# A two-level Strassen-Winograd channel MLP: the transposes of its input move from TensorE to VectorE

## The chip, the cores and the metric

The kernel runs on one core of one Trainium2 chip. A core has TensorE (PE: matmuls, and weight loads shown as PEld), VectorE (DVE), ScalarE (ACT), GpSimd (POOL), SyncE (SP, which only issues transfers here) and 16 DMA engines. The metric is the device time of one execution in microseconds (us), the median of several runs.

## The reference, cut to what matters

All data are fp32. Attention without softmax over 8 batches, 8 heads, 576 tokens and 64 columns a head gives x; then a token-mixing MLP and a channel MLP follow:

```
kv  = einsum('bhsd,bhse->bhde', k, v)
o   = einsum('bhsd,bhde->bhse', q, kv)
x   = o / sqrt(mean(o*o) + 1e-6) * g_norm           # heads side by side: (8, 576, 512)
u   = x + (relu(x.T @ w_tok1) @ w_tok2).T            # w_tok1 (576, 256), w_tok2 (256, 576)
out = u + relu(u @ w_ch1) @ w_ch2                    # w_ch1 (512, 1536), w_ch2 (1536, 512)
```

The change is in the last line, the channel MLP, which fills most of the time.

## The kernel before, in words

**First pass.** Attention and token mixing run over pairs of batches. VectorE meanwhile decodes the weights (rounds of small integer and float steps). The result u goes to DRAM in nine groups of 512 tokens by 512 columns (`u_dram[0..8]`): the first 512 tokens of each batch, and a ninth group of the 64 left over of all eight.

**Second pass.** For each group, `channel1` forms v = relu(u @ w_ch1) and `channel2` adds v @ w_ch2 to u. Both products use the Strassen-Winograd scheme: 7 block products in place of 8, with sums of blocks before and after. For group 0 one level is used (`channel1_once`, `channel2_once`), and at the same time VectorE makes the sums of weight blocks that the later groups need, and they are stored in DRAM. For groups 1 to 8 two levels are used: 7 outer products, each of 7 inner ones. An inner product is three matmuls of 128x128x128.

**Places.** The order of groups 1 to 8 is written by hand. An inner product has a place, a whole number: outer product number n starts at place 7n, and its inner products 1, 2, 6, 5, 7, 4, 3 stand at 7n + 0, 1, 3, 4, 6, 9, 12 (`PLACE`), so that consecutive outer products interlock and each place has one inner product. A group takes 14 outer products, so 98 places: a cycle. Everything else is put beside a place with `put`: the loop at the end of the kernel emits the product of a place and then what stands beside it, and each engine keeps this program order. `channel2` of a group begins 49 places after its `channel1`; in the text, places count from the start of `channel1`'s cycle, and `b` in the code is the first place of the half concerned.

**Banks of an outer product** (`outer`). Inner products 1, 6, 7 and 4 add up in PSUM bank "a". Between them the bank is read: t1 after 1, u2 after 6, u3 after 7, the result (1,0) after 4. Such a read is a copy by ACT, or, where a block of another outer product is to be added (`base`), an add by VectorE. Product 2 has bank "c", 5 and 3 share bank "b"; VectorE adds t1, u2, u3 to them (`write`).

**Sums.** `inner(o)` makes the sums of v's blocks that outer product o of `channel2` needs (tiles sv, sv3; VectorE). S1 to S4 and A21 (`sum1` to `sum4`, `make_a21`) are the outer sums of v, each in two halves of 768 elements. `radd` and `xadd` gather the result tiles r into xg, which holds u and becomes the output. POOL makes two of v's outer sums. `fetch_sums` loads the weight sums of outer product n + 3 after product n (three buffers).

**Transposes.** The channel product needs u with columns on partitions. `fetch_t` loads 128 tokens of a group, `turn_u` transposes them by four TensorE transposes into PSUM (`ps_ut`, line 515) and ACT copies them into uT. For group g + 1 that happens within `channel2` of g, at its places 11, 15, 19 and 23. `outer_u` and `inner_u` then form the sums of uT's blocks (VectorE).

**Queues.** In the second pass all transfers are issued by SyncE, in program order.

Of the kernel before, what the change touches and what calls it, by code (L numbers as in the profile page):

```python
# [19 lines left out]
def kernel(  # L20
# [481 lines left out]
    def fetch_t(g, i):  # L502

        if g < NG:
            xt[g, i] = late["xt"].tile([P, DM], F32, name="xt")
            dma(xt[g, i], u_dram[g][ts(i, P)])

    def turn_u(g, i, psum):
        if g >= NG:
            return  # L510
        if i == 0:
            uT[g] = late["u"].tile([P, 7, 7, P], F32, name="uT")
        pt = psum()
        for c in range(NC):
            keep(nc.tensor.transpose(pt[:, c], xt[g, i][:, ts(c, P)], ident))  # L515
        o, n = 2 * (i // 2), 2 * (i % 2)
        copy(uT[g][:, o:o + 2, n:n + 2], pt.rearrange("p (o n) t -> p o n t", o=2))

    def outer_u(g):

        return t_sums(lambda n: uT[g][:, SB[n], :4]) if g < NG else []

    def inner_u(g, lo, hi):

        return t_sums(lambda n: uT[g][:, lo:hi, SB[n]]) if g < NG else []
# [5 lines left out]

    def t_psum():
        return late["t"].tile([P, NC, P], F32, name="ps_ut")
# [20 lines left out]
    def channel1_once(g):  # L554
# [4 lines left out]
        def pair(d):  # L559
            a11, a12, a22, s1, s2, s3, s4 = (t[:, 2 * d:2 * d + 2] for t in blocks)  # L560
            shape = [P, 2, 2, P]

            def product(n, ps, start, stop):
                for w in range(2):
                    i, f = divmod(2 * d + w, W)
                    for c in range(2):
                        wt = w_ch1[:, SA[n]] if SA[n] < 4 else late["w2"][:, SA[n] - 4]
                        matmul(ps[:, w], lhsT=wt[:, 2 * i + c, ts(f, P)],
                               rhs=uT[g][:, SB[n], c:4:2],
                               start=(start and w == 0 and c == 0), stop=stop,  # L570
                               skip_group_check=True)

            at = {}

            def first():
                for n in ("t1", "u2", "u3"):
                    at[n] = r_tile().rearrange("p i (j t) -> p i j t", j=2)
                for n in (1, 6, 7, 5):
                    at[f"p{n}"] = m_psum(shape, f"ps_v{n}")
                product(1, at["p1"], True, False)  # L580
                copy(at["t1"], at["p1"])

            def sixth():
                product(6, at["p6"], True, True)
                tensor_add(at["u2"], at["p6"], at["t1"])

            def seventh():
                product(7, at["p7"], True, False)
                tensor_add(at["u3"], at["p7"], at["u2"])

            def fifth():
                product(5, at["p5"], True, False)
                tensor_add(a22, at["p5"], at["u3"])
                relu(a22, a22)

            def second():
                product(2, at["p1"], False, True)
                relu(a11, at["p1"])

            def fourth():  # L600
                product(4, at["p7"], False, True)
                tensor_add(a12, at["p7"], at["u2"])
                relu(a12, a12)

            def third():
                product(3, at["p5"], False, True)
                tensor_add(s3, at["p5"], at["u2"])
                v_sums(s1, s2, s3, a11, a22)
                v_sum3(s3, a11)
                tensor_add(s4, a12, s2, ALU.subtract)  # L610

            return [first, sixth, seventh, fifth, second, fourth, third]
# [63 lines left out]
    def outer(place, size, mul, to, base=None):  # L676
# [11 lines left out]
        def temp(n, bufs):  # L688
            t[n] = late["tmp"].tile([P, FQ], F32, name=n, tag=n, bufs=bufs)[:, :size]
            return t[n]  # L690

        def fit(flat, like):
            return flat if len(like.shape) == 2 else flat.rearrange("p (w t) -> p w t", w=W)

        def read(o, i, j):

            a = fit(banks["a"], to(i, j))
            o = fit(o, to(i, j)) if len(o.shape) == 2 else o
            if base:
                tensor_add(o, a, base(i, j))  # L700
            else:
                copy(o, a)

        def write(i, j, name, n):
            o = to(i, j)
            tensor_add(o, fit(banks[name], o), fit(t[n], o))
# [30 lines left out]
    ORDER1, ORDER2 = (1, 6, 2, 7, 5, 3, 4), (1, 4, 6, 5, 7, 2, 3)  # L737
# [3 lines left out]
    def fetch_sums(n):  # L741
        if n < len(order):
            w, _, o = order[n]
            sums[n] = sums_tile()
            dma(sums[n], sums_dram[w, o])
# [6 lines left out]
    def channel1(g, n0):  # L752
# [4 lines left out]
        def first(i, o):  # L757
            n = n0 + i

            def mul(p, ps, start, stop):  # L760
                for w in range(W):
                    matmul(ps[:, ts(w, P)], lhsT=part(1, o, p, sums[n])[:, ts(w, P)],
                           rhs=uT[g][:, SB[o], SB[p]], start=(start and w == 0), stop=stop,
# [18 lines left out]
        put(b + 24, *add(3, 3, 1))  # L782
        put(b + 36, *add(1, 4, 3, nc.gpsimd))
        put(b + 43, *add(7, 5, 4, nc.gpsimd))
        for t, *places in ((2, 25, 29, 28, 25), (7, 47, 47, 48, 48), (1, 53, 57, 53, 54)):
            for place, (i, j) in zip(places, ((0, 0), (0, 1), (1, 0), (1, 1))):
                rectify(place, t, i, j)
        if g > 1:
# [4 lines left out]
    def channel2(g, n0):  # L793
# [3 lines left out]
        def second(i, o):  # L797
# [15 lines left out]
            outer(7 * n, P, mul, to)  # L813
# [3 lines left out]
        rs = {o: second(i, o) for i, o in enumerate(ORDER2)}  # L817

        def inner(o):
# [24 lines left out]
            return begin, steps[1], own if o == 1 else steps[2], steps[3]  # L844
# [5 lines left out]
        def sum1(i):  # L850
            keep(nc.vector.scalar_tensor_tensor(out=half(n5(), i), in0=half(a21(), i), scalar=0.0,
                                                in1=half(n4(), i), op0=ALU.max, op1=ALU.add))

        def sum2(i):
            tensor_add(half(n6(), i), half(n5(), i), half(n1(), i), ALU.subtract)

        def sum3(i):

            keep(nc.vector.scalar_tensor_tensor(out=half(n7(), i), in0=half(a21(), i), scalar=0.0,
                                                in1=half(n1(), i), op0=ALU.max, op1=ALU.subtract))  # L860

# [12 lines left out]
        for place, steps in (  # L874
                (-17, [ins[1][0], ins[1][2]]), (-16, [ins[1][1]]), (-14, [ins[1][3]]),
                (1, [A[0], ins[4][0]]), (2, [A[1]]), (4, [ins[4][1], S1[0]]), (6, [ins[4][3], S1[1]]),
                (7, [ins[4][2]]), (8, [S2[0]]), (9, [S2[1]]), (11, [ins[6][0]]), (12, [S4[0]]),
                (13, [ins[6][1], S4[1]]), (15, [ins[6][3], ins[6][2]]), (17, [ins[5][0], S3[0]]),
                (19, [ins[5][1], S3[1]]), (20, [xadd(0, 0, 1)]), (21, [ins[5][3], ins[5][2]]),
                (23, [ins[7][0], xadd(1, 0, 4)]), (25, [ins[7][1]]), (26, [ins[7][2], ins[7][3]]),  # L880
                (28, [ins[2][0]]), (29, [radd(6, 1)]), (30, [ins[2][1], xadd(0, 1, 6)]),
                (32, [ins[2][3], ins[2][2]]), (34, [ins[3][0]]), (36, [xadd(0, 1, 5), ins[3][1]]),
                (37, [xadd(1, 1, 5)]), (38, [ins[3][3], ins[3][2]]), (43, [radd(7, 6)]),
                (44, [xadd(1, 0, 7)]), (45, [xadd(1, 1, 7)])):
            put(b + place, *steps)

        if g < NG - 1:
            for place, steps in ((57, [do(store, g, xg, 1)]), (59, [xadd(0, 0, 2)]), (63, [xadd(0, 1, 3)]),
                                 (71, [do(store, g, xg, 0)]), (78, [do(fetch_x, g + 1, 0)]),
                                 (85, [do(fetch_x, g + 1, 1)])):  # L890
                put(b + place, *steps)
        else:
# [5 lines left out]
            put(b + 49, xadd(0, 0, 2), do(store, g, xg, 1))  # L898
# [5 lines left out]
        for i in range(J):  # L904
            place = b + 12 + 4 * i
            put(place - 12, do(fetch_t, g + 1, i)) if i < 2 else None
            put(place - 1, do(turn_u, g + 1, i, t_psum))
            put(place, do(fetch_t, g + 1, i + 2)) if i < 2 else None

        if g + 1 < NG:  # L910
            first, second, _, fourth = inner_u(g + 1, 0, 2)
            put(b + 40, first)
            put(b + 41, second)
            put(b + 42, fourth)
# [129 lines left out]
    late["xt"] = pool("xt", 2)  # L1044
    late["u"] = pool("u", 1)
    fetch_t(0, 0)
# [4 lines left out]
    def turn(g, i, psum):  # L1051
        turn_u(g, i, psum)
        if i + 2 < J:
            fetch_t(g, i + 2)

    u_psum = lambda: ps["o"].tile([P, NC, P], F32, name="ps_ut", tag="o")
    last = [
        "h00 2 -s40 2", "h01 2", "h10 2", "h11 2", "hr 1", "c0 u0 1", "c1 u1 1", "c2 u2", "c3 u3 1", "u4",
        "c4 u5 1", "u6 1", "u7", "u8"]
    more = {f"c{i}": do(turn, 0, i, u_psum) for i in range(J)}  # L1060
# [5 lines left out]
    right.close()  # L1066
    late["v"] = pool("v", 1, "right")
    late["r"] = pool("r", 4, "right")
# [5 lines left out]
    late["m"] = pool("m", 6, space=bass.MemoryType.PSUM)  # L1074
    late["t"] = pool("t", 2, space=bass.MemoryType.PSUM)
# [4 lines left out]
    fetch_t(1, 0)  # L1080
    fetch_t(1, 1)
# [3 lines left out]
    weave(channel1_once(0), firsts + [f for fs, _ in inner1 for f in fs])  # L1085
    for n in range(3):
        fetch_sums(n)
    extra = [do(turn, 1, i, t_psum) for i in range(J)]
    extra += [lambda: [f() for f in outer_u(1)], lambda: [f() for f in inner_u(1, 0, 7)], lambda: None]
    body = [step for pair in zip(channel2_once(0), extra) for step in pair]  # L1090
# [50 lines left out]
```

## Time and profile before

| | |
|---|---|
| time, median of 3 runs | 831.82 us (831.56 to 831.87) |
| profiled span | 830.2 us |
| second pass, from its first two-level product | 281 us to the end |
| one cycle (groups 1 to 7) | 67.8 us |
| VectorE busy in a cycle | 58.44 us |
| DMA share in a cycle | 0.52 |

Each line of the page's list of groups gives source line, engine, operation, output and inputs, shape and count, then busy us, mean ns of one, and idle time of the engine before them. As most operations are recorded by a few helpers, many groups share a line (127 matmul, 118 tensor_add, 124 copy); tile names tell them apart. An fp32 matmul shows as two records, a transpose as one. "Busy" counts overlapping instructions once, and a mean duration includes the latency that the next instruction overlaps; the price of an instruction in a full queue is the distance between starts.

### The profile page before, as it was taken

The numbers are of one execution on the slowest core, as the hardware profiler recorded it, in microseconds if no ns is written. First come the engines' busy times: TensorE is split into PE (matmuls) and PEld (weight loads), VectorE is DVE, ScalarE is ACT, GpSimd is POOL, SyncE is SP. The second block draws the span as 40 slices with busy tenths as digits, with TensorE's granted clock in tenths as the row PEclk, the third lists the DMA queues.
The fourth block names the chain that finished last, engine by engine and source line by source line (L and its number), as shares of the span: only waits on it lengthen the run. The fifth ranks groups of instructions, "written<-read, shape, count | busy, mean of one in ns | idle before, by whom it ended". The sixth has DMA issues, their size and how long they took to land.

```text
span 830.2 us, 16562 instructions
## 1 busy us (share of the span) xinstructions
PE 812.6 (98%) x6528; PEld 719.9 (87%) x6528; DVE 701.8 (85%) x1334; ACT 289.1 (35%) x777; POOL 76.9 (9%) x59
## 2 busy tenths in 40 slices
PE   6999999999999999999999999999999999999997
PEld 6655555644888899999999999999999999999997
DVE  4688989999785979978977987997897897798696
ACT  1346665562210124234234323322423322333321
POOL 1200101010000020003003003001100300300300
PEclk9999999999999999999999999999999999999999
DMA  9999996422436445365356446546536545644642
GB/s 296 325 341 319 337 364 244 153 89 102 174 127 220 175 169 170 118 194 200 128 165 216 144 141 204 181 140 193 192 115 191 185 149 145 216 164 141 190 144 80
DMA packets 67966, 156.57 MB, mean 189 GB/s; under 512 B 5296, under 2 KB 24752, under 8 KB 67888
## 3 DMA queue, kind: packets, MB, share of 16 engines
q1 hardware_dynamic: 66208, 153.77, 56.6%
q10 hardware_dynamic: 1680, 1.74, 0.7%
q8 instruction: 52, 0.85, 0.4%
q14 instruction: 26, 0.21, 0.1%
HBM read 128.35 MB, written 27.13 MB: 187 GB/s over the span
## 4 chain that ended last, share of the span: by engine, by line
PE 88%; DVE 9%; issue 1%; DMA 1%; ACT 1%; SPq 0%; ACTq 0%; DVEq 0%
PE ps_a L127 35%; PE ps_b L127 18%; PE ps_c L127 9%; PE ps_h L127 6%; PE ps_u L127 6%; PE ps_v L127 4%; PE ps_w L127 3%; PE ps_o L127 3%; PE ps_ut L515 2%; PE ps_kv L127 2%; DVE sv L118 1%; DMA raw<-in_moe_w_tok_dram 1%; DVE v L118 1%; DVE x L379 1%; DVE ms L399 1%
## 5 line engine op out<-in xcount | busy, mean ns | idle before, releaser
L124 ACT COPY u<-ps_a 128x128 f32<-128x128 f32 (+1 forms) x176 | 60.5, 344 | 176.5 <-PE ps_a L127 164.6
L118 POOL TENSOR_TENSOR v<-v,v 128x768 f32<-128x768 f32 x32 | 58.4, 1856 | 553.0 <-ACT t L124 553.0
L127 PE MATMUL ps_b<-uT,sums 128*128 128x128 f32 x672 | 85.5, 275 | 0.0
L127 PEld LDWEIGHTS ps_b<-uT,sums 128*128 128x128 f32 x672 | 80.2, 192 | 0.0
L127 PE MATMUL ps_a<-uT,w_ch 128*128 128x128 f32 x576 | 78.8, 275 | 0.0
L127 PEld LDWEIGHTS ps_a<-uT,w_ch 128*128 128x128 f32 x576 | 71.5, 192 | 0.1
L118 DVE TENSOR_TENSOR v<-ps_b,u 128x384 f32<-128x384 f32 x112 | 60.2, 550 | 12.9 <-PE ps_b L127 12.9
L127 PE MATMUL ps_u<-h,w_tok 128*128 128x512 f32 (+1 forms) x160 | 67.0, 601 | 0.0
L127 PE MATMUL ps_h<-x,w_tok 128*128 128x512 f32 (+1 forms) x160 | 65.8, 603 | 0.8 <-ACT x L424 0.8
L118 DVE TENSOR_TENSOR v<-v,v 128x768 f32<-128x768 f32 (+1 forms) x70 | 64.1, 926 | 0.3
L118 DVE TENSOR_TENSOR uT<-uT 128x512 f32<-128x512 f32 (+4 forms) x103 | 63.1, 628 | 1.1
L124 ACT COPY t<-ps_a 128x128 f32<-128x128 f32 (+1 forms) x88 | 30.3, 344 | 92.7 <-PE ps_a L127 85.3
L121 ACT ACTIVATE v<-v 128x384 f32<-128x384 f32 (+1 forms) x102 | 49.3, 526 | 30.7 <-DVE v L118 26.6
L127 PE MATMUL ps_a<-uT,w 128*128 128x128 f32 x432 | 58.7, 275 | 0.0
L118 DVE TENSOR_TENSOR u<-ps_a,v 128x384 f32<-128x384 f32 x48 | 26.8, 558 | 32.1 <-PE ps_a L127 31.6
L127 PEld LDWEIGHTS ps_h<-x,w_tok 128*128 128x128 f32 (+1 forms) x160 | 25.9, 189 | 31.9 <-issue 28.1
L127 PEld LDWEIGHTS ps_a<-uT,w 128*128 128x128 f32 x432 | 53.4, 192 | 0.0
L118 DVE TENSOR_TENSOR xg<-xg,r 128x512 f32<-128x512 f32 (+1 forms) x78 | 50.7, 661 | 0.8 <-ACT r L124 0.6
L424 ACT ACTIVATE x<-x,inv 128x64 f32<-128x64 f32 x184 | 46.0, 335 | 9.5 <-DVE inv L419 8.1
L127 PE MATMUL ps_a<-uT,sums 128*128 128x128 f32 x336 | 46.9, 276 | 1.3 <-ACT t L124 1.3
L127 PE MATMUL ps_a<-sums,sv 128*128 128x128 f32 x336 | 47.3, 277 | 0.9 <-ACT r L124 0.5
L127 PEld LDWEIGHTS ps_u<-h,w_tok 128*128 128x128 f32 (+1 forms) x160 | 24.5, 179 | 27.1 <-issue 22.4
(123 smaller groups left out, 1650.1 us busy)
## 6 DMA issues: line engine op xcount, KB each, us to landing
sums<-sums SPq DMA_DIRECT2D x112, 576.0 KB, 3.8
qT<-in_q_dram SPq DMA_DIRECT2D x8, 1152.0 KB, 9.5
xt<-u_dram SPq DMA_DIRECT2D x36, 256.0 KB, 3.5
xg<-u_dram SPq DMA_DIRECT2D x18, 512.0 KB, 4.9
k_in<-in_k_dram SPq DMA_DIRECT2D x16, 512.0 KB, 9.2
u_dram<-x SPq DMA_DIRECT2D x16, 512.0 KB, 3.6
out_dram<-xg SPq DMA_DIRECT2D x16, 512.0 KB, 5.4
sums<-sv SPq DMA_DIRECT2D x14, 576.0 KB, 2.8
```

The lines of the kernel that those rows point to most:

```text
L118: keep(engine.tensor_tensor(out=o, in0=a, in1=b, op=op))
L121: keep(nc.scalar.activation(o, a, AF.Relu))
L124: keep(nc.scalar.copy(o, a))
L127: keep(nc.tensor.matmul(*a, **kw))
L379: keep(nc.vector.tensor_mul(heads(X[pair, c][:, t]), heads(bank[c, t]), g_sb.to_broadcast([P, H, D])))
L399: keep(nc.vector.tensor_reduce(stats_of(c)[0][:, ts(t, H)], sq[c, t], axis=AX.X, op=ALU.add))
L424: keep(nc.scalar.activation(x[:, i], x[:, i], AF.Copy, scale=inv[:, i]))
L515: keep(nc.tensor.transpose(pt[:, c], xt[g, i][:, ts(c, P)], ident))
```

## The change

It takes the 36 x 4 transposes from TensorE. VectorE transposes blocks of 32x32 instead (two instructions for each of four quarters of a group), four transfers a quarter put these blocks into DRAM, and eight transfers a group bring them back so that the blocks stand as a whole transpose in uT. Rows of uT are thus split in four pieces of 32 tokens, and matmuls and sums read them so. The loads for it run far ahead: quarters are turned during `channel1` of the group before.

To make room on VectorE, the outer products of `channel2` come in the order 1, 2, 4, 7, 6, 5, 3 (before: 1, 4, 6, 5, 7, 2, 3), and those of `channel1` have 4 before 3. S3 is made first, S2 from S3, S1 from S2. Product 6 adds product 1's result as it reads its bank, which saves one `radd`. There are five result tiles in place of four; seven of the result additions, and the stores, move to the beginning of the next cycle. POOL makes one of its sums in quarters. The two PSUM banks of the transposes go to the products (8 in place of 6). The loads of weight sums are issued by ACT.

```diff
-            xt[g, i] = late["xt"].tile([P, DM], F32, name="xt")
-            dma(xt[g, i], u_dram[g][ts(i, P)])
+            xt[g, i] = late["xt" if g else "xt0"].tile([P, 2, DH], F32, name="xt")
+            dma(xt[g, i], u_dram[g].rearrange("(t p) e -> p t e", p=P)[:, ts(i // 2, 2), ts(i % 2, DH)])
-        for c in range(NC):
-            keep(nc.tensor.transpose(pt[:, c], xt[g, i][:, ts(c, P)], ident))
-        copy(uT[g][:, o:o + 2, n:n + 2], pt.rearrange("p (o n) t -> p o n t", o=2))
+        for t in range(2):
+            keep(nc.vector.transpose(
+                y[:, :, 2 * t:2 * t + 2].rearrange("p b n t -> p n b t"),
+                xt[g, i][:, t].rearrange("p (n b t) -> p n b t", n=2, b=NC)))
+        for a in range(NC):
+            dma(blocks_dram[g, half][:, :, o, a], y[ds(a * Q, Q)].rearrange("p b n t -> p b (n t)"))
+    def fetch_u(g, half):
+            uT[g] = late["u"].tile([P, 7, NC, 7, Q], F32, name="uT")
+        for b in range(NC):
+            dma(uT[g][ds(b * Q, Q), 2 * half:2 * half + 2, :, :4].rearrange("p o a n t -> p o a (n t)"),
+                blocks_dram[g, half][:, b])
...
-    ORDER1, ORDER2 = (1, 6, 2, 7, 5, 3, 4), (1, 4, 6, 5, 7, 2, 3)
+    ORDER1, ORDER2 = (1, 6, 2, 7, 5, 4, 3), (1, 2, 4, 7, 6, 5, 3)
-            dma(sums[n], sums_dram[w, o])
+            dma(sums[n], sums_dram[w, o], nc.scalar)
+        for place, f, i in ((18, turn_blocks, 0), (19, fetch_t, 1), (29, turn_blocks, 1), (30, fetch_t, 2),
+                            (40, turn_blocks, 2), (41, fetch_t, 3), (49, turn_blocks, 3), (70, fetch_t, 4)):
+            put(b + place, do(f, g + 1 + i // J, i % J))
+            outer(7 * n, P, mul, to, o == 6 and (lambda i, j: rs[1][0][:, i, ts(j, P)]))
...
+                (8, [A[0]]), (9, [A[1]]), (10, [ins[2][3]]), (11, [S3[0]]), (12, [S3[1]]),
+                (14, [ins[4][2]]), (15, [S2[0]]), (16, [ins[4][3]]), (17, [ins[7][0]]), (18, [xadd(0, 0, 1)]),
+                (19, [ins[7][1]]), (21, [S2[1], ins[7][2]]), (23, [ins[7][3]]), (24, [S1[0]]),
+            for place, steps in ((45, [xadd(0, 1, 6)]), (48, [radd(7, 6)]), (57, [xadd(1, 1, 5)]),
+                                 (59, [xadd(1, 0, 4)]), (60, [xadd(1, 0, 7)]), (61, [xadd(1, 1, 7)]),
+                                 (61, [do(store, g, xg, 1)]), (63, [xadd(0, 1, 5)]), (64, [xadd(0, 1, 3)]),
+                                 (66, [do(store, g, xg, 0)]), (74, [do(fetch_x, g + 1, 0)]),
...
+        put(b + 8, do(fetch_u, g + 1, 0))
+        put(b + 12, do(fetch_u, g + 1, 1))
-    late["r"] = pool("r", 4, "right")
+    late["r"] = pool("r", 5, "right")
-    late["m"] = pool("m", 6, space=bass.MemoryType.PSUM)
-    late["t"] = pool("t", 2, space=bass.MemoryType.PSUM)
+    late["y"] = pool("y", 1, "right")
+    late["m"] = pool("m", 8, space=bass.MemoryType.PSUM)
```

## The prediction

> **What bounds the kernel now.** I read the page's busy table and slices first, then the chain that ended last, then PE's timeline by stage, then VectorE's load by stage, then the transfers.
>
> ```profile
> PE 812.6 (98%) x6528; PEld 719.9 (87%) x6528; DVE 701.8 (85%) x1334; ACT 289.1 (35%) x777; POOL 76.9 (9%) x59
> ...
> PE 88%; DVE 9%; issue 1%; DMA 1%; ACT 1%; SPq 0%; ACTq 0%; DVEq 0%
> ```
>
> ```profile
> L515 PE MATMUL ps_ut<-ident,xt 128*128 128x128 f32 x144 | 21.7, 273 | 0.0
> ```
>
> ```profile
> 248.05 0.44 PE ps_ut L515 x4
> ```
>
> TensorE never rests and is 88% of the chain, so its instruction count sets the time. The second fence is the group of the 144 transposes (busy us, mean ns, idle before); the third is one entry of the chain in order of time (start, us): four transposes hold TensorE for 0.44 us. Their mean of 273 ns is a pipelined latency, not a price.
>
> The second pass repeats in cycles, one for each of groups 1 to 8. TensorE's timeline, around the transposes of one cycle:
>
> ```profile
> 457.05 0.83 PE L127 MATMUL ps_b<-sums,sv 128*128 128x128 f32 x6
> 457.72 0.60 PE L515 MATMUL ps_ut<-ident,xt 128*128 128x128 f32 x4
> 458.16 0.93 PE L127 MATMUL ps_b<-w_ch,sv 128*128 128x128 f32 x6
> 458.92 1.50 PE L127 MATMUL ps_a<-d,v 128*128 128x128 f32 x12
> ...
> 461.37 0.83 PE L127 MATMUL ps_a<-sums,v 128*128 128x128 f32 x6
> 462.25 0.91 PE L127 MATMUL ps_a<-sums,sv 128*128 128x128 f32 x6
> ```
>
> Columns: start, us, engine, line, operation, count, idle before and who ended it. A product of the inner scheme (a "place": three fp32 matmuls, six records) starts every 0.67 us. A cycle is 98 places x 0.67 = 65.68, plus 16 transposes at 4 x 0.435 = 1.74, plus starts that come late: 462.25 is 0.88 after 461.37 (0.21 lost), and the gaps after 458.16 and 462.25 are 0.76 and 0.75 (0.09, 0.08 lost). Sum 67.80, the period seen.
>
> The second engine is VectorE (DVE), by stretches of one such cycle:
>
> ```profile
> 387.00:407.40 20.40, 20.35 (x182) 20.11 (x181) 20.36 (x42) 6.89 (x21) 0.00 (x0) 1.00 0.49 161
> 353.40:387.00 33.60, 33.60 (x303) 33.60 (x302) 25.35 (x49) 12.18 (x28) 7.29 (x4) 1.00 0.61 198
> ```
>
> Columns: stretch, length, then busy us of PE, weight loads, DVE, ACT, POOL, clock, DMA share, GB/s. DVE is full (20.36 of 20.40) in the first part of the second product and has 8 us free in the first product. What that fullness costs is seen in the last cycle, which has no transposes in it:
>
> ```profile
> 797.11 0.94 PE L127 MATMUL ps_b<-w_ch,sv 128*128 128x128 f32 x6 [0.27 <-DVE r L118]
> ...
> 801.22 0.91 PE L127 MATMUL ps_a<-sums,sv 128*128 128x128 f32 x6 [0.49 <-ACT r L124]
> ```
>
> TensorE loses 0.43, 0.66 and 0.63 us there (starts against the 0.67 step), with 0.09 after each: 2.0 us. So taking the transposes out and nothing else would give back in stalls what it saves: 1.74 + 0.38 a cycle against 2.0. The reordering is the part that decides.
>
> **What the Trainium skill says.** "Perfetto Trace Analysis", Identifying the Most-Contended Engine, says that matmul busy overstates how full TensorE is and weight-load busy is better: here 98% and 87%, and the unbroken 0.67 us step agrees that nothing is left but to issue fewer instructions. "VectorE: DVE Perf Modes", The three transpose paths, says that VectorE transposes blocks of 32x32 only; hence the detour of the blocks through DRAM, which no trace here shows yet. "DMA: Bandwidth & Descriptors", Issuing engines are not separate DMA queues, says that loads issued by ACT share the engines with SyncE's and only save issue time; not shown before, since the second pass issues all on SyncE.
>
> **The change, part by part.**
>
> *Transposes and their copies leave TensorE and ACT.* 36 x 0.44 = 15.8 us on the path. With them goes the wait of 0.38 a cycle, in the seven cycles that have it: 2.7 us. 36 ACT copies (587 ns) go too; ACT is 35% busy, worth nothing by itself.
>
> *VectorE's load.* DVE prices from starts that follow each other:
>
> ```profile
> 796.30 0.55 DVE L118 TENSOR_TENSOR v<-v 128x384 f32<-128x384 f32 x1
> 796.77 0.28 DVE L118 TENSOR_TENSOR r<-ps_b,u 128x128 f32<-128x128 f32 x1
> 796.97 0.95 DVE L118 TENSOR_TENSOR v<-v,v 128x768 f32<-128x768 f32 x1
> 797.84 0.28 DVE L118 TENSOR_TENSOR r<-ps_c,t 128x128 f32<-128x128 f32 x1
> ```
>
> 384 elements occupy 0.47, 128 0.20, 768 0.87: 1.04 ns an element and 68 ns. A block transpose (8 a cycle, 256 elements of a partition each) is not in the trace. "Vector Engine (DVE) Microarchitecture Reference", 3.8 The reshape front-end, gives one element per cycle per lane: 0.34 us by the same line, my value. Upper bound 0.60, if four-byte data took two passes. A cycle gains 8 x 0.34, four adds of 128 in place of ACT copies in product 6 (0.80), and loses one add of 512 (0.60): 56.6 to 59.4 of 65.7 us.
>
> I laid each DVE instruction at the place where the code puts it and summed by stretch. Places 49 to 76 (second product, first part): before 20.8 us for 18.8 of matmuls and 1.7 of transposes; after 17.7 for 18.8. Seven result additions leave for places 8 to 15 of the next cycle, and S3, S2, S1 are spread over places 60 to 77. Places 7 to 27: before 10.5, after 13.6 of 14.1. So the stretch that starved TensorE is relieved, and the free one nearly filled. The last cycle's 2.0 us should go.
>
> *Where DVE now can hold TensorE.* Products 2, 5, 4 (and now 6) are read out of bank "a" by DVE, and the same bank is wanted three places later: 1.34 us, less the read's 0.56 and some 0.1 of hand-over, leaves 0.69 us of lateness. Following DVE's queue from place to place with these prices, the latest such reads are u2 at places 17 and 38, 0.6 us late: just inside. At 0.60 a transpose, place 38 is 1.05 late: 0.36 a cycle. I charge 0.15 x 8 = 1.2 us.
>
> *New waits.* DVE's transpose waits for its load (3.5 us median) and for the 4 stores of the one before, since there is one buffer of each; behind it in DVE's queue stand the writes and reads that TensorE's banks wait for. Transposes are 9 to 11 places (6 to 7.4 us) apart; 1.7 us of stores' issue and the load fit with 0.6 to 1 us over. The last one, at place 49, may be 0.7 late, where the reads that follow are ACT's. The eight loads of uT may start at place 57 at the earliest and are first needed at place 91: some 20 us, against 4 + 4 transfers of 3 to 5 us that overlap. ACT now issues the 14 loads of sums, each after the copy of u3; behind it stands the next copy of "a", 2 us later, and an issue is 0.32 us on SyncE. The sums (3.8 us to landing) have 11 places, 7.4 us, less that copy.
>
> *First pass and entry.* Eight transposes for group 0 (2.7 us) fall where DVE is 90% busy; sums of uT move behind u7. 0.5 us charged. The gap at the entry to the steady part:
>
> ```profile
> 285.74 0.83 PE L127 MATMUL ps_a<-uT,w_ch 128*128 128x128 f32 x6
> 287.86 0.94 PE L127 MATMUL ps_a<-uT,sums 128*128 128x128 f32 x6 [1.29 <-ACT t L124]
> ```
>
> is 1.45 us, and 0.1 after it: DVE's backlog of uT sums. They now come one product (5.6 us) earlier, into idle time of DVE. I count 1.0 us of it as gained.
>
> Five result tiles and eight PSUM banks let results live across the cycle; ordering 3 and 4 swapped costs nothing as long as POOL's four quarter sums (about 0.95 us each, half of 1856 ns) end before product 4 reads them, 1.3 us earlier by the same count. S1 and S2 from S3 are as many instructions of the same price.
>
> Sum: 15.8 + 2.7 + 2.0 + 1.0 - 1.2 - 0.5 = 19.8 us; 831.8 - 19.8 = 812.0.
>
> **Rivals.**
> *VectorE takes over.* For: 59.4 of 65.7 us, and 0.09 us in hand at place 17. Against: lateness stays under 0.69 up to a transpose of about 0.4. At 0.60, 0.36 x 8 = 2.9 us more: 815; at 1.0 (64.8 of 65.7) reads are 2.7 late, 2 us a cycle: 828.
> *The detour and the queues.* u goes out and in again, 2 MB a cycle in pieces of 512 bytes, DMA share 0.52 before. ACT's loads reuse semaphores of SyncE's transfers, and an ACT held there delays copies. If half of the gain of a cycle is lost so, 1.2 x 8: 822.
> *Slower.* If the sums land 1 us late for four products a cycle, 4 x 8 = 32: 844. If matmuls that read uT in pieces of 32 columns ran 10% longer (half of all, 32.8 us a cycle), 3.3 x 8 = 26: 838. Against both: 3.8 us against about 7, and pieces of 128 with gaps (ps_v, 380 ns for 256 columns) show no cost now.
>
> **How the numbers follow.** Forecast (809 to 815.5) 0.64; VectorE 0.17; queues 0.10; slower 0.07; below the 809.7 that is left if nothing is charged and all of the entry's gap goes (831.8 - 15.8 - 2.7 - 2.0 - 1.6), 0.02. The range runs from 808.5 to 822, taking in most of the first two rivals. Faster 0.91 and same 0.02, since a bad case of the queues can eat the whole gain; slower 0.07.
>
> **What would show it.** Right: period 65.7 to 66.0 us, no ps_ut, transposes near 0.34 from start to start, no PE wait for DVE at places 49 to 76. Wrong: a PE wait repeated each cycle on DVE u2 (places 17, 38), on DMA sums, or a step over 0.67 us for products on uT.

## The result and the profile after

The changed kernel takes 842.4 us (median of four runs, 838.2 to 844.7) against 831.7 before: 1.0123 times as long, 95% interval 1.0082 to 1.0163. The prediction was 812.0, faster. The profiled run took 838.2. The page of the changed kernel, busy table, then the chain that ended last, by engine and by line:

```profile
PE 807.2 (97%) x6384; PEld 707.4 (85%) x6384; DVE 730.0 (87%) x1430; ACT 255.1 (31%) x709; POOL 78.9 (9%) x75
...
PE 52%; DVE 28%; DMA 11%; issue 4%; SPq 4%; ACT 0%; ACTq 0%; DVEq 0%
PE ps_a L127 20%; PE ps_b L127 9%; DMA xt<-u_dram 6%; DVE uT L118 6%; PE ps_c L127 5%; PE ps_h L127 5%; DVE xg L118 4%; DVE v L118 4%; SPq L115 4%; PE ps_u L127 4%; DVE sv L118 3%; PE ps_w L127 2%; PE ps_o L127 2%; DVE r L118 2%; DMA v_in<-in_v_dram 2%
```

The 144 matmul records of the transposes are gone, and TensorE is still "97% busy". But its share of the chain fell from 88% to 52%: 28% of it is now VectorE's, and 11% that of transfers, first among them the load of xt, which was on no path before. The waits of VectorE (total us, times, longest) name it, and the group of the new transposes (busy, mean ns, idle before) shows how much:

```profile
DVE y L520 <- DMA xt<-u_dram: 25.3, 16, 4.0
```

```profile
L520 DVE STREAM_TRANSPOSE y<-xt 128x256 f32<-128x256 f32 x72 | 27.6, 421 | 28.5 <-DMA xt<-u_dram 25.3
```

They stand still as long (28.5 us) as they work.

Where the time went, from TensorE's starts (each start against the one before, less the 111.7 ns of an unhindered matmul record; that step is the same before and after, also for products on uT):

| part of the span | before | after | difference |
|---|---|---|---|
| 144 transposes, 109 ns each | 15.7 | 0 | -15.7 |
| TensorE's late starts from the first product of ps_a on | 7.2 | 22.4 | +15.2 |
| length of the ps_v part (first products of group 0) | 36.4 | 40.6 | +4.3 |
| last start of TensorE to the end | 4.9 | 6.9 | +2.0 |
| sum | | | +5.8 |

The span grew from 830.2 to 836.1 us, 5.9. The other three runs of the changed kernel, 3.9 to 6.5 us longer, were not profiled; their granted TensorE clock was 0.996, 0.996 and 0.993, against 0.999 in this one, which would be 5 of the 6.5 us in the longest (an estimate from these figures: 0.006 of 838 us).

In the repeated part the gaps sit at fixed products. They are counted here by TensorE's products from the start of a cycle; the places in the code and in the prediction are two higher, so product 18 is the code's place 20. In us a cycle: 0.71 at products 17 and 18 (in all cycles but the first), 1.0 at 36 to 39, 0.24 at 50. Irregular ones come at 32, 42, 52 and 71 (5.7 us in all). One cycle (start, us, operation, count, idle before and its cause; count the start against 0.67 us a product):

```profile
498.62 0.83 PE L127 MATMUL ps_b<-uT,sums 128*128 128x128 f32 x6
499.64 0.94 PE L127 MATMUL ps_b<-uT,sums 128*128 128x128 f32 x6 [0.19 <-DVE v L118]
500.57 1.60 PE L127 MATMUL ps_a<-uT,w_ch 128*128 128x128 f32 x12
```

```profile
513.00 0.94 PE L127 MATMUL ps_a<-uT,sums 128*128 128x128 f32 x6
513.78 1.66 PE L127 MATMUL ps_b<-uT,sums 128*128 128x128 f32 x12
515.89 0.94 PE L127 MATMUL ps_a<-uT,w_ch 128*128 128x128 f32 x6 [0.46 <-DVE u L118]
```

From 498.62 to 499.64 are 1.02 us for one product; from 513.78 to 515.89 are 2.11 for two. The cause named at these products is VectorE, never a transfer. VectorE's timeline of the second stretch:

```profile
508.48 0.77 DVE L520 STREAM_TRANSPOSE y<-xt 128x256 f32<-128x256 f32 x2 [0.55 <-DMA xt<-u_dram]
...
512.40 0.55 DVE L118 TENSOR_TENSOR t<-ps_a,v 128x384 f32<-128x384 f32 x1
512.87 1.11 DVE L118 TENSOR_TENSOR sv<-v,sv 128x384 f32<-128x384 f32 x1
...
515.29 0.54 DVE L118 TENSOR_TENSOR u<-ps_a,v 128x384 f32<-128x384 f32 x1
517.02 0.77 DVE L520 STREAM_TRANSPOSE y<-xt 128x256 f32<-128x256 f32 x2 [1.18 <-DMA xt<-u_dram]
```

Two things are to be seen. The transposes at the head of the queue wait for xt, and an addition of 384 elements takes 1.11 us where it takes 0.55 elsewhere. GpSimd's timeline beside it:

```profile
512.56 0.99 POOL L118 TENSOR_TENSOR v<-v,v 128x384 f32<-128x384 f32 x1 [2.60 <-DVE v L118]
```

VectorE's addition starts 0.31 us into this quarter sum and ends 0.42 after it. All eight meetings of this kind look alike (1.10 to 1.12 us). Five other additions of 384 elements with both inputs in SBUF (sv<-v), which start 0.43 to 0.85 us into a quarter sum, take 0.57 to 0.98 us, and they too end 0.41 to 0.42 us after it: the end follows from GpSimd's end, whenever they start. VectorE's instructions that read PSUM keep their 0.55 us beside GpSimd, and the transposes stay below 0.45.

Why xt is late is in SyncE's queue (start, time in issue, count):

```profile
706.51 2.49 SPq L115 DMA_DIRECT2D blocks<-y  x4
709.04 0.59 SPq L115 DMA_DIRECT2D xt<-u_dram  x1
```

The load of the next xt is put behind the four stores of the last blocks. These take 2.5 us to issue and xt another 4 to land: the last transposes began at 705.72, and the next ones could not before 713.50.

### The profile page after: what moved, and what is told of

Read it like the earlier page. It is cut to its first block, busy times and chain, and to the rows that moved or that the text cites. A ratio compares the mean times of both kernels' runs of the same rounds, so it can differ in the third digit from the quotient of the medians.

```text
span 836.1 us, 16599 instructions
## 1 busy us (share of the span) xinstructions
PE 807.2 (97%) x6384; PEld 707.4 (85%) x6384; DVE 730.0 (87%) x1430; ACT 255.1 (31%) x709; POOL 78.9 (9%) x75
## 3 DMA queue, kind: packets, MB, share of 16 engines
q1 hardware_dynamic: 95008, 106.59, 41.9%
## 4 chain that ended last, share of the span: by engine, by line
PE 52%; DVE 28%; DMA 11%; issue 4%; SPq 4%; ACT 0%; ACTq 0%; DVEq 0%
PE ps_a L127 20%; PE ps_b L127 9%; DMA xt<-u_dram 6%; DVE uT L118 6%; PE ps_c L127 5%; PE ps_h L127 5%; DVE xg L118 4%; DVE v L118 4%; SPq L115 4%; PE ps_u L127 4%; DVE sv L118 3%; PE ps_w L127 2%; PE ps_o L127 2%; DVE r L118 2%; DMA v_in<-in_v_dram 2%
## 5 line engine op out<-in xcount | busy, mean ns | idle before, releaser
L118 POOL TENSOR_TENSOR v<-v,v 128x384 f32<-128x384 f32 (+1 forms) x48 | 60.4, 1274 | 558.5 <-DVE v L118 558.5
L124 ACT COPY u<-ps_a 128x128 f32<-128x128 f32 (+1 forms) x160 | 56.0, 350 | 176.2 <-PE ps_a L127 166.3
L127 PE MATMUL ps_b<-uT,sums 128*128 128x128 f32 x672 | 88.7, 277 | 1.3 <-DVE v L118 1.3
L127 PE MATMUL ps_a<-uT,w_ch 128*128 128x128 f32 x576 | 80.7, 279 | 4.0 <-DVE u L118 3.7
L124 ACT COPY t<-ps_a 128x128 f32<-128x128 f32 (+1 forms) x80 | 28.0, 350 | 173.7 <-PE ps_a L127 156.9
L118 DVE TENSOR_TENSOR v<-v,v 128x768 f32<-128x768 f32 (+1 forms) x86 | 79.9, 929 | 0.6
L520 DVE STREAM_TRANSPOSE y<-xt 128x256 f32<-128x256 f32 x72 | 27.6, 421 | 28.5 <-DMA xt<-u_dram 25.3
L127 PEld LDWEIGHTS ps_h<-x,w_tok 128*128 128x128 f32 (+1 forms) x160 | 25.9, 189 | 31.0 <-issue 28.5
```

Of the source, the lines that this page charges most:

```text
L118: keep(engine.tensor_tensor(out=o, in0=a, in1=b, op=op))
L124: keep(nc.scalar.copy(o, a))
L127: keep(nc.tensor.matmul(*a, **kw))
L520: keep(nc.vector.transpose(y[:, :, 2 * t:2 * t + 2].rearrange("p b n t -> p n b t"), xt[g, i][:, t].rearrange("p (n b t) -> p n b t", n=2, ...
```

## The experiments

Each kernel is the changed one with the edit shown, unless it says otherwise; each time is a median, with a ratio to the kernel before measured beside it. Places in edits are the code's; where the expectations speak of a gap at a place, they mean the count of products used above. The changed kernel's own median is known to about 3.4 us (its interval), so a difference to it of less than about 4 us is not settled by the times, and the gaps in the traces are then the evidence.

**The next load ahead of the stores, in the loop.**

```
     def turn_blocks(g, i, nxt=None):
...
+        if nxt:
+            fetch_t(*nxt)
         if o == 0:
             blocks_dram[g, half] = ...
```

> In the loop the load of the next xt is issued ahead of the four stores of the blocks instead of behind them; everything else as in the changed kernel (842.4 us). Theory A (VectorE stands at the head of its queue for a load that comes too late): the waits of the transposes for xt (0.3 to 1.8 us at the second, 1.1 at the third, 1.8 to 2.4 at the fourth) fall to nearly nothing, the TensorE gaps at places 32 and 42 go, the one at place 39 (0.62 us) shrinks to about 0.3, and the time falls by 5 to 8 us, to 834 to 837. Theory B (VectorE has simply too much to do): the gaps at 17, 36 to 39 stay as they are and the time stays within 2 us of 842.

837.5 us, ratio 1.0076 (1.0059 to 1.0092): 4.9 less, just under theory A's 5 to 8 (in the traces the late starts fell by 3.5). The irregular gaps at 42, 52 and 71 fell from 3.7 us in all to 0.4, those at 32 only from 2.0 to 1.6; 36 to 39 stayed (8.0 us in both), so there the theory's share of xt was wrong. VectorE's transposes have a new wait:

```profile
  DMA blocks<-y: 7.4, 12
  DMA xt<-u_dram: 7.2, 3
```

(what it waited for: us, times). The one buffer of y is next: the stores of the last blocks must land before it is written again. The three waits for xt left are all in the part that runs once.

**The same, in the part that runs once.** There each load stands one step ahead of its transposes, about 4 us.

```
-    blocks1 = [do(f, 1, i) for f, i in (
-        (fetch_t, 0), (turn_blocks, 0), (fetch_t, 1), (turn_blocks, 1), ...
+    blocks1 = [do(fetch_t, 1, 0), lambda: None] + [
+        do(turn_blocks, 1, i, (1, i + 1) if i < 3 else (2, 0)) for i in range(J)]
```

> Only in the part that runs once, for group 1: each load of xt is issued one step (about 4 us) earlier, with the transposes before it, ahead of their stores. Theory: the two transposes there that waited 2.5 and 4.0 us for their load held TensorE for 4.2 us in the products of ps_v (40.8 us against 36.5 before the change); they no longer wait, the ps_v part is 36.5 to 37 us long, and the time falls by about 4 us, to 838. Rival: the transposes' own 2.9 us on VectorE are what costs there, and 2 us or more of the 4.2 stay.

836.6 us, 1.0057 (1.0042 to 1.0072): 5.8 less, more than expected. The part is 36.37 us long, the length before the change, though its eight transposes are still in it. So this term was the wait alone. Why its removal was worth more than the 4.3 us of the profiled run can be seen in the seven other traces that keep the wait (e1, e4, e6 to e9, x1): right behind it, TensorE's clock is granted at half for 3.41 us (the ps_v records start every 427 ns instead of 216), and the part is 41.9 to 43.0 us long. In the changed kernel's profiled run this did not happen. The changed kernel, VectorE and then TensorE:

```profile
229.88 0.77 DVE L520 STREAM_TRANSPOSE y<-xt 128x256 f32<-128x256 f32 x2 [4.00 <-DMA xt<-u_dram]
```

```profile
231.28 1.99 PE L127 MATMUL ps_v<-uT,w 128*128 128x256 f32 x8 [3.50 <-DVE v L118]
```

One wait of 4.0 us at the head of VectorE's queue became 3.5 us of TensorE, through a VectorE addition queued behind it.

**The detour left out.**

```
     def turn_blocks(g, i):
-        if g >= NG:
+        if g > 1:
             return
```

(the loads of xt and uT likewise)

> Leaves out, for groups 2 to 8, the loads of xt, the transposes, the stores and the loads of uT; uT of group 1 is used again. The new order, five result tiles and the part that runs once stay. Theory: the gap at places 17 and 18 (0.7 us a cycle) stays, since seven result additions that were moved to places 8 to 15 fill VectorE ahead of it; the gaps at 32 to 42 go, and so do the ones on sums at place 71, as the transfers halve; 824 to 829 us. If the new order itself were the loss, the time would stay above 836; if all of it were the detour, it would fall to 818 or below (842.4 less 22 of gaps in the loop, tail and once part left).

834.2 us, 1.0029 (1.0019 to 1.0039). The expectation missed by 5 to 10 us. The gaps at 32, 42 and 71 went as forecast, but those at 36 to 39 did not, although no transpose and no transfer of the detour was left in these cycles. TensorE in this kernel:

```profile
564.83 0.83 PE L127 MATMUL ps_b<-uT,sums 128*128 128x128 f32 x6
565.85 0.94 PE L127 MATMUL ps_b<-uT,sums 128*128 128x128 f32 x6 [0.19 <-DVE v L118]
...
579.75 1.66 PE L127 MATMUL ps_b<-uT,sums 128*128 128x128 f32 x12
581.87 0.94 PE L127 MATMUL ps_a<-uT,w_ch 128*128 128x128 f32 x6 [0.46 <-DVE u L118]
```

The same waits to 0.01 us. Products 17, 18, 36 to 39 and 50 lose 15.0 us in eight cycles here and 14.9 in the changed kernel. This is the new order, not the detour, and not the time of the transposes on VectorE either.

**The kernel before, without its transposes.**

```
     def turn_u(g, i, psum):
-        if g >= NG:
+        if g > 1:
             return
```

> The kernel before without the transposes of groups 2 to 8, their loads and their copies (uT of group 1 is used again); its order stays. The prediction said that this alone gives back in stalls what it saves: 67.68 us a cycle instead of 67.80, 831 us. Rival: the last cycle's stalls (2.0 us) belong to that cycle alone and the others would gain all of 1.74 a cycle: 831.8 - 12.2 = 819.6 us.

831.0 us, 0.9991 (0.9984 to 0.9997), as forecast. The stalls that only the last cycle had are now in every one:

```profile
457.58 0.94 PE L127 MATMUL ps_b<-w_ch,sv 128*128 128x128 f32 x6 [0.27 <-DVE r L118]
461.68 0.91 PE L127 MATMUL ps_a<-sums,sv 128*128 128x128 f32 x6 [0.49 <-ACT r L124]
468.45 0.94 PE L127 MATMUL ps_b<-d,sv 128*128 128x128 f32 x6 [0.46 <-DVE r L118]
```

So in the old order TensorE's transposes were almost free (0.7 us). Beside e4 this prices the new order by itself: without transposes for groups 2 to 8 the repeated part, from the first product of ps_a to TensorE's last start, is 542.3 us in the new order and 543.9 in the old. It takes away 16.9 of 18.8 us of late starts and makes 15.2 of its own. (As a whole e4 is 3.2 us slower, since the waits of the part that runs once and the longer end are still in it.)

**One quarter sum of GpSimd less.**

```
-        for place, i, j in ((25, 0, 0), (30, 1, 1), (31, 1, 0), (35, 0, 1)):
+        for place, i, j in ((25, 0, 0), (30, 1, 1), (31, 1, 0)):
```

> Leaves out one of the four quarter sums on GpSimd in each cycle (v1 = v4 + v3 for its last quarter, place 35), so v1 is wrong there; nothing else changes. In the changed kernel the VectorE addition sv<-v,sv that meets this sum takes 1.10 us instead of 0.55 and ends 0.42 after the sum does. Theory A (a VectorE addition whose inputs are both in SBUF waits until GpSimd's addition is over): it takes 0.55 again, the gap at place 39 falls from 0.62 to about 0.1, 8 x 0.5 = 4 us, 842.4 to 838. Theory B (VectorE is late there because of its own queue): the duration may fall, but the gap stays above 0.4 and the time within 1 us of 842.

839.8 us, 1.0106 (1.0083 to 1.0129): 2.6 less, not 4, and by the times alone not settled. VectorE's addition is back at its old time:

```profile
514.05 0.55 DVE L118 TENSOR_TENSOR sv<-v,sv 128x384 f32<-128x384 f32 x1
```

and the gaps at 38 and 39 fell from 7.0 to 2.5 us, somewhat more than the 4 us of theory A, though 0.32 us a cycle stay at 39. 2.0 of it came back at 42, where a transpose waits for xt.

**One result addition moved, with the store and the load behind it.**

```
-                                 ... (64, [xadd(0, 1, 3)]),
-                                 (66, [do(store, g, xg, 0)]), (74, [do(fetch_x, g + 1, 0)]),
+                                 ... (72, [xadd(0, 1, 3)]),
+                                 (73, [do(store, g, xg, 0)]), (81, [do(fetch_x, g + 1, 0)]),
```

> One of the seven result additions that the change put into places 8 to 15 (the one of product 3) goes to place 23, its store to 24 and the load behind it from 25 to 32. Theory: VectorE comes 0.6 us earlier to the reads and writes at places 15 to 17, the gaps at places 17 and 18 (0.71 us a cycle, seven cycles, 5.0 us in all) fall to 1 us or less in all, and the time from 842.4 to 838. Rival: the gap moves to places 20 to 26, and the time stays within 1 us.

835.3 us, 1.0048 (1.0028 to 1.0069): 7.1 less. No gap at 17 and 18 is left (5.0 us before), and none at 32 (2.0 before). In all, its trace has 6.0 us fewer of late starts.

**Rectifications behind the copies.**

```
-        for t, *places in (..., (7, 47, 47, 48, 48), ...):
+        for t, *places in (..., (7, 51, 51, 52, 52), ...):
```

> The four rectifications of v7 on ScalarE go from places 47 and 48 to 51 and 52, behind the copies of bank a of the second product's first places. Theory: the gap at place 50 (0.24 us a cycle, 1.9 us in all) is ScalarE's queue of seven rectifications ahead of the copy of t1, and goes; 842.4 to 840.5. Rival: it is the copy's own latency behind the product, and stays.

841.9 us, 1.0123 (1.0101 to 1.0145): unclear by the time, but the gap at 50 is gone in all cycles (1.9 us to 0), while those at 32 and 52 are 2.7 us larger in the profiled run, and 1.0 us is new at 78.

**Sums issued by SyncE again.**

```
-            dma(sums[n], sums_dram[w, o], nc.scalar)
+            dma(sums[n], sums_dram[w, o])
```

> The 14 loads of sums of a cycle are issued by SyncE, as before the change, not by ScalarE. Theory A (ScalarE held on semaphores shared with SyncE's transfers costs time): the holds of up to 3.1 us before its copies go, and the time falls by 1 to 3 us. Theory B (SyncE's queue is the narrow one): the loads queue behind the stores of the blocks, the gaps at places 32 and 71 on xt and sums grow, and the time rises by 3 us or more.

859.3 us, 1.0324 (1.0299 to 1.0349): theory B, and far beyond it, though the gaps stand at 29, 52 and 71 (10.7, 5.8 and 6.5 us) and the one at 32 shrank. TensorE's waits in this kernel, then SyncE's for TensorE here and in the changed kernel:

```profile
PE ps_a L127 <- DMA sums<-sums: 13.9, 14, 2.5
```

```profile
SPq L115 <- PE ps_a L127: 170.0, 60, 5.0
```

```profile
SPq L115 <- PE ps_a L127: 1.9, 5, 0.5
```

The move to ScalarE's queue is worth 17 us beside this detour. The prediction took it to save the time of issue only; the traces show that on SyncE's queue everything behind these loads also waits with them for TensorE. How much of the 17 us is due to either was not separated. In the kernel before, SyncE waited so for 177.0 us without such a cost, with no detour in its queue.

**The four sums of the second product's first operand moved.**

```
-                (-17, [ins[1][0], ins[1][2]]), (-16, [ins[1][1]]), (-14, [ins[1][3]]),
+                (-10, [ins[1][0], ins[1][2]]), (-9, [ins[1][1]]), (-8, [ins[1][3]]),
```

> The changed kernel with one edit: the four sums sv of the second product's first operand at places 39 to 41 instead of 32 to 35; all of the computation stays. Theory: the gaps at places 36 to 39 (1.0 us a cycle) go, since VectorE has four additions fewer ahead of the reads of product 4 and none of them meets GpSimd's quarter sums: 842.4 - 8 = 834.5; at most 1 us comes back at place 42. If only the meeting with GpSimd counts, the gap at 39 keeps 0.1 to 0.2 and 36 keeps 0.1, and 838 comes out as in e7_no_quarter.

842.2 us, 1.0137 (1.0115 to 1.0160): nothing gained, and the expectation was wrong. The gaps at 36 to 39 are gone, and 8.3 us stand at 42 (1.4 before): the sums, with the third transposes among them, now hold another read of bank a.

**All of it together, and two further spacings.** x2 joins e1, e2, e8, e9 and x1, leaves the last stores to SyncE and makes the addition that one of them waits for a place earlier. x3 then moves the fourth transposes from place 49 to 52, and the second half of the loads of uT from 61 to 67.

> The changed kernel with its losses mended together: each load of xt ahead of the stores (in the loop and in the part that runs once), one result addition moved from place 15 to 23, the rectifications of v7 behind the first copies of the second product, the four sums sv of the second product's first operand moved from places 32 to 35 to places 39 to 41 (away from GpSimd's quarter sum and from the reads of product 4), and at the end the last stores issued by SyncE instead of ScalarE. Theory (these are separate losses, each by its place): 842.4 - 5.8 (once) - 5.0 (17, 18) - 8 (36 to 39) - 1.9 (50) - 2 (end) - 2 to 4 (waits for xt) = 816 to 818 us, below both kernels. If a loss only moves to the next full stretch of VectorE, the sum will not add up and the time stays above 825.

> As x2_all, with the cycle's last transposes at place 52 instead of 49 and the second half of the loads of uT at place 67 instead of 61. Theory: the one buffer of y is then free in time (with the loads ahead, the transposes waited up to 1.2 us for the landing of the stores of y), a further 0.5 to 2 us less than x2_all. Rival: VectorE has no room at 52, and it is slower than x2_all by 1 us or more.

x2: 824.7 us, 0.9912 (0.9897 to 0.9927). x3: 821.1 (820.5 to 821.3), 0.9871 (0.9859 to 0.9884), the best of all, 1.3% below the kernel before, with the transposes on VectorE. The sum that I expected of x2 did not add up by 7 to 9 us: 5.5 us are left at 42 (x1's), 5.3 at 71. The end is hardly better either (6.6 us). x3 gained more than expected (3.6 us): the waits of the fourth transposes for y, up to 2.3 us in x2, fell to 0.6 at most, and the gaps at 71 to 1.1 us in all. Which of its two moves did this was not separated. x3's page:

```profile
PE 66%; DVE 21%; DMA 6%; issue 3%; SPq 3%; ACT 1%; DVEq 0%; ACTq 0%
```

TensorE has 66% of the chain again, not 88. The late starts are 10.2 us, of them 5.7 at 42.

> As x3_later_turn, with the third pair of transposes at place 45 instead of 40 and the fourth at 54 instead of 52, and with half of the stores before the last issued by GpSimd instead of SyncE. Theory: the gap at place 42 (5.7 us in all in x3_later_turn) comes from the third transposes and the four moved sums standing together ahead of the read of bank a at place 41, part of it from xt landing late; with 5 places more it goes to under 1 us, and VectorE has 0.7 us without work near place 45: 821.1 - 4 to 5 = 816 to 817. The end (6.6 us behind TensorE's last product) shortens by 0 to 2 us. Rival: the loads follow each other too closely behind place 54, the gaps at 71 on sums grow, and nothing is gained.

831.5 us, 0.9996 (0.9988 to 1.0005): 10 us slower than x3. The gap at 42 is gone, the end is 0.9 us shorter, but 9.2 us stand at 57 and 4 at 59 and 66. One more kernel takes the two moves of transposes apart:

> As x3_later_turn, with the third pair of transposes two places later (42 instead of 40, behind the read of bank a at 41) and the fourth left at 52; half of the stores before the last issued by GpSimd, which shortened the end by 0.9 us in x5_spread_pool_store. If the gap at place 42 (5.7 us in all) is the third transposes standing ahead of that read, it goes, the places 57 to 73 stay as in x3_later_turn, and the time is 821.1 - 5 to 6 = 815 to 816 us. If the ten places between the third and the fourth are too few for the stores of y (x5: nine, with waits of 0.5 to 2.8 us), a gap of about 1 us a cycle opens at 52 to 59 and the time is 821 or more.

824.7 us, 0.9917 (0.9903 to 0.9930). Both branches of the expectation hold: the gap at 42 was the third transposes standing ahead of the read (5.7 us to nothing), and new gaps opened behind the fourth, though of half the size named (4.1 us in all at 57 and 59, and 2.2 at 66). VectorE's waits on the stores of y in x6, then in x3:

```profile
DVE y L520 <- DMA blocks<-y: 21.6, 9, 3.3
```

```profile
DVE y L520 <- DMA blocks<-y: 5.5, 7, 1.4
```

Ten places after the third transposes the one buffer of y is still being stored, and the fourth wait at the head of the queue in VectorE's full stretch; with twelve places they hardly do. A second buffer of y might separate the two; it was not tried.

## Why the prediction was wrong, by its steps

*Right.* Removing 144 transposes is worth 15.7 us (forecast: 15.8). A VectorE transpose takes 0.36 to 0.37 us from start to start (forecast: 0.34). The step stays 0.67 us on pieces of 32 columns. Removing the transposes alone gains almost nothing (e5). The stretch that starved TensorE is relieved: between products 53 and 98 only the gap at 71, in three of the cycles, is left, and one of 0.6 in the last cycle that was there before. ScalarE as issuer of the sums stood among the rivals and is a gain (e6).

*Wrong, first: "the latest such reads are u2 at places 17 and 38, 0.6 us late: just inside"*, charged at 1.2 us for eight cycles. Both reads start later: 1.35 us after their product at 17 and 1.52 at 38, against the 0.69 that can be borne. This costs 5.0 and 8.0 us. At 17 VectorE comes with a backlog from places 8 to 15, where six result additions stand now (two before the change; the seven named above are a miscount); one fewer (0.6 us) and the gap is gone (e8), and the first cycle, which has none of them, has no gap there. At 38, 0.55 us of the lateness is the meeting with GpSimd, which the sum had at nothing: "ordering 3 and 4 swapped costs nothing as long as POOL's four quarter sums end before product 4 reads them". They end in time, and hold VectorE while they run. e7 took that away and 4.5 of 7.0 us at 38 and 39 with it; the rest is VectorE's own queue, and goes when the four sums of the second product's first operand are moved (x1). The Trainium skill has this in "SBUF — State Buffer", Who interferes with whom: a VectorE instruction with two inputs in SBUF contends with a GpSimd one that reads SBUF, the port that they share is an exclusive lock, and the order of issue decides who blocks. The trace agrees (1.10 us instead of 0.55, ending 0.42 after the sum), also in that VectorE's reads of PSUM are not touched. My step looked only at when the sums end. Late reads at places 17 and 38 are what the prediction named as its first sign of being wrong. Its rival "VectorE takes over" came true, but not for the reason it gives: the transposes did not take 0.60 us, and without them the gaps are the same (e4).

*Second: "1.7 us of stores' issue and the load fit with 0.6 to 1 us over."* The four stores take 2.5 us to issue, and the load behind them lands about 7 us after the transposes, not 5.2. Waits of up to 1.8 us at the second and third transposes and 1.2 to 2.4 at the fourth followed; putting the load first is worth 4.9 us by the times and 3.5 by the late starts (e1).

*Third: "first pass and entry ... 0.5 us charged".* The eight transposes of group 0, which the step priced, cost nothing seen. Those of group 1, which it did not, waited 2.5 and 4.0 us for their loads: 4.3 us in the profiled run, 5.8 by e2, where the stretch at half clock behind the wait goes too. Of the 1.0 us at the entry 0.65 was gained.

*Left out.* That a stall of TensorE can bring its clock down for a while was in no term (some 1.7 us behind the wait in ps_v, in the seven traces named at e2). ScalarE, whose relief was called "worth nothing by itself" by its share, had seven rectifications in one row ahead of a copy (1.9 us at 50, e9). At the end, the stores on ScalarE's queue wait for a late addition, and a copy of TensorE's bank waits behind them (2.0 us). ScalarE issued these four stores before the change too (the second pass was not all on SyncE), but then they were in time:

```profile
829.21 1.46 ACTq L115 DMA_DIRECT2D out_dram<-xg  x2
830.70 0.27 ACT L124 COPY r<-ps_a 128x128 f32<-128x128 f32 x1 [2.81 <-issue]
```

This reading of the end is argued from the trace: x2 and x3, which put these stores on SyncE, had the copy in time and an end only 0.2 us shorter, as SyncE's own stores then queue.

Together, against the forecast: 11.8 us (13.0 less the 1.2 charged) at 17 to 39, 3.8 (4.3 less 0.5) in the first part, 5.7 at the irregular places, 1.9 at 50, 2.0 at the end, 0.35 at the entry make 25.6 of the 26.2 us by which the profiled run missed 812.0. The 4.2 us from there to the median of 842.4 lie in runs that were not profiled.

## What to carry over

When an engine that sets the pace is relieved by one that is 85% busy, ask of each stretch how late the second engine comes to the buffers that the first wants back, and carry its backlog from one stretch into the next: a mean of 59 us of work in a cycle of 66 said nothing about 0.7 us at two places. An instruction that waits for a transfer belongs on an in-order queue only where nothing urgent stands behind it, and its load ahead of, not behind, the stores of the last round. And moving a block of work out of one full stretch is a gain only if the place where it lands has room: x1 gave back all that it took, and x5 more than that.

## What the runs showed of the hardware

- A VectorE addition with both inputs in SBUF, started within a GpSimd addition, waits until that is over: 1.10 us instead of 0.55 in the eight meetings of one kind, 0.57 to 0.98 in five of another, and in all thirteen the end is 0.41 to 0.42 us after GpSimd's. GpSimd's own time was 0.99 to 1.01 us. In the kernel before the same pair met in the other order: VectorE, first by 0.25 us, kept its 0.55, and GpSimd's half sum shows as 1.97 us in the profile, against 1.82 for the same form in the changed kernel; that it waited meanwhile is inferred.
- A store of 64 KB from y, in pieces of 512 bytes, takes about 0.6 us to issue on SyncE (median of 144): the four shown take 2.5 us, on the path of whatever stands behind.
- A stall of TensorE can cost more than its length. Where a ps_v record starts 3.7 to 4.0 us after the one before it, seven of eight traces show TensorE's clock granted at half for the next 3.41 us, with steps of 427 ns in place of 216, and one (the changed kernel's) does not. In x2 the same stretch comes 0.4 us behind a stall of 2.1 us (steps of 213 ns in place of 112); in e8 none follows one of 2.3 us.
